# Retention and a gated FFN on one Trainium2 core: g tiles in fourteen places, and smaller last accumulators

## The chip, the core and the metric

The kernel runs on one core of one Trainium2 chip. The metric is device time in microseconds (us); the kernel before takes 590.42 us (median of 3 runs, 590.29 to 590.98). Engines are named as the profile names them: PE (matrix multiply), DVE (vector), ACT (scalar), POOL (GpSimd), SP (the queue that issues nearly all DMAs). Each engine works through its own list of instructions in order, and waits where an instruction's inputs, or the place it writes, are not ready.

## The reference

Attention without softmax, as a recurrence with one decay per head, then two matrix products with a relu6 gate between them:

```python
gamma = 1.0 - 2.0 ** (-5.0 - np.arange(H))
for t in range(S):                       # B, H, S, D = 4, 8, 768, 64
    state = gamma * state + k[:, :, t] (x) v[:, :, t]
    y[:, :, t] = q[:, :, t] @ state / sqrt(D)
x = y as (B*S, H*D) = (3072, 512)
h = x @ w_in                             # w_in 512 x 2048, float64
g = h * clip(h + 3, 0, 6) / 6
out = g @ w_out                          # w_out 2048 x 512, float64
```

All outputs are float32. Both weights come as float64, and have to be turned into float32 on the chip.

## The kernel before

**First phase.** The 3072 tokens are six units (0 to 5) of 512. For each unit, attention makes x, kept as a rounded part and a remainder, so that a product of two such numbers takes three matmuls. Then 16 tiles jj of h are made, one for each 128 columns of w_in: `mm1(u, jj)` does 12 matmuls of 128x512 (4 blocks k, 3 products) into a PSUM tile `h` (three of them in turn), ACT and DVE turn h into `g` (128x512, L468 and L469), and SP stores g to `gd` in DRAM (L470).

**Second phase.** `out` is made with a seven-product scheme (Strassen's, in Winograd's form) over pairs of token tiles and halves of w_out. There are three blocks `sb` of 1024 tokens, each with four groups g of products: (4, 5), (1, 6), (7), (2, 3). A group goes through four steps c: SP loads a tile `gv` of stored g, DVE adds or subtracts into `spare`, ACT and DVE split the operand into its two parts `gc` (L140 and L141), and PE multiplies it by `w2c[2c]` and `w2c[2c + 1]` (L587), 12 matmuls for each product. A step of the first group has two products, so 24 matmuls.

**Weights.** `build_w1` (16 of them) and `build_w2` (16 halves, two for each of the eight tiles w2c[0] to w2c[7]) fetch float64 words into `st` (two buffers), make float32 of them with the five DVE instructions on L122, L123, L128, L131 and L134 and one ACT instruction (L126), with `wb`, `we` and `ww` in one buffer each. A half of w2 then takes four small sums `ws` (L93) and two splits: ACT writes the rounded part into the tile (L140), DVE the remainder (L141), for three blocks from `ww` and four from `ws`. The table WHEN says after which tile of h a half stands in the program: three halves in unit 1, three in unit 2, two each in units 3 and 4, six in unit 5.

**Places.** `wpool` has ten large slots of 14 KB per partition: one of its own ("w0": the first part of w1, later w2c[5]) and nine in rotation ("w"). In program order these hold the early loads of q, k, v and of a decay table, the other four parts of w1, two tiles with x of unit 2, the tiles of w2 and, in the second phase, two `spare`. A tile may be written once the reads of the tile before it in that slot are over. A part of w1 holds 14 of the 64 blocks (jj, k); it is read in every unit, for the last time in unit 5. Part 1 holds blocks 14 to 27, so its last use is jj = 6, k = 3.

**Order.** Only PE's order is written out by hand (`manual_schedule`). The order on the other engines is made when the program is built, by a scheduler that puts an instruction where it expects its inputs and its place to be ready. Second-phase pools lie where the first phase's were: the second `gv` buffer lies over the two `st`, the third over `wb`, `we`, `ww` and `ws`.

Of the kernel before, what the change touches and what calls it, by code (L numbers as in the profile page):

```python
# [19 lines left out]
P = 128  # L20
# [8 lines left out]
def retention_ffn(ctx: ExitStack, tc: tile.TileContext, qkv, w_in, w_out, dvs, dqs, dkc, dqc, dmc, out, B, H, S, D):  # L29
# [14 lines left out]
    UR = 4  # L44
# [96 lines left out]
        nc.vector.tensor_tensor(out=lo, in0=src, in1=hi, op=ALU.subtract)  # L141


    w1s = {}

    def place(shape, dtype, name, own):

        return wpool.tile(shape, dtype, tag="w0" if own else "w", name=name, bufs=1 if own else NSLOT - 1)

    def w1_block(j, k):  # L150
        s, o = divmod(j * NK + k, 14)
# [45 lines left out]
    def load(r):  # L197

        t = rows[r] = {}
        if r < AHEAD and r % 2 == 0:
            early[r] = wpool.tile([P, 7, NPAIR, P], F32, tag="w", name=nm("early"), bufs=NSLOT - 1)
        for i, (x, n) in enumerate((("kt", 1), ("qt", 0), ("vn", 3), ("kn", 2))):
            o = r % 2 * 4 + i
            if r < AHEAD and o < 7:
                t[x] = early[r // 2 * 2][:, o]
            elif x == "kn" and r > CHUNKED and r % 2:
                t[x] = both["am"][:, 1]  # L210
            else:
                tag = SPARE[r // 2] if r < AHEAD else f"l{x}"
                t[x] = apool.tile([P, NPAIR, P], F32, tag=tag, name=nm(x), bufs=BUFS[tag])
            m = NPAIR * P
            if x == "kn" and r % ROWS_B == ROWS_B - 1:
                m = m // 2 if r >= CHUNKED else 0
            if m:
                nc.sync.dma_start(out=t[x].rearrange("p h n -> p (h n)")[:, 0:m], in_=qkv[r, n][:, 0:m])
        if r >= CHUNKED:
            t["vn"], t["kn"] = (  # L220
                t[x].rearrange("p h n -> p (h n)").rearrange("p (c a e) -> p c a e", c=2, e=D) for x in ("vn", "kn")
            )
            scale(r)
        elif r >= AHEAD:
            decay(r)
# [23 lines left out]
    def load_decay(r):  # L249
        if r < AHEAD:  # L250
            if "dq" not in early:
                early["dq"] = wpool.tile([P, ROWS_B, NPAIR, P], F32, tag="w", name=nm("early"), bufs=NSLOT - 1)
            t = early["dq"][:, r % ROWS_B]
        else:
            t = apool.tile([P, NPAIR, P], F32, tag="dq", name=nm("dq"), bufs=1)
        rows[r]["dq"] = t
        if r < ROWS_B or r >= AHEAD:
            nc.sync.dma_start(out=t.rearrange("p h n -> p (h n)"), in_=dqs[r % ROWS_B])
# [75 lines left out]
    def x_place(r):  # L334
        u, n = divmod(r, UR)
        if u not in xs and u == 2:
            xs[u] = [wpool.tile([P, NK, UT], F32R, tag="w", name=nm("x"), bufs=NSLOT - 1) for a in range(2)]
        elif u not in xs:
            x = xpool.tile([P, 2, NK, UT], F32R, tag="x", name=nm("x"))
            xs[u] = [x[:, a] for a in range(2)]  # L340
        return [xs[u][a][:, :, n * P : (n + 1) * P] for a in range(2)]
# [117 lines left out]
    def mm1(u, jj):  # L459
        h = ps_h.tile([P, UT], F32, tag="h", name=nm("h"))  # L460
        for k in range(NK):
            t, o = w1_block(jj, k)
            for n, (a, b) in enumerate(((0, 0), (0, 1), (1, 0))):
                nc.tensor.matmul(  # L464
                    h, t[:, o, a], xs[u][b][:, k], start=k + n == 0, stop=(k, n) == (NK - 1, 2), skip_group_check=True
                )
        g = hpool.tile([P, UT], F32, tag="g", name=nm("g"))
        nc.scalar.activation(out=g, in_=h, func=AF.Relu, bias=three)  # L468
        ins = nc.vector.scalar_tensor_tensor(out=g, in0=g, scalar=6.0, in1=h, op0=ALU.min, op1=ALU.mult)  # L469
        nc.sync.dma_start(out=gd[jj // 2][:, jj % 2, u * UT : (u + 1) * UT], in_=g)  # L470
        return ins.ins
# [10 lines left out]
    for n, (u, jj) in enumerate(steps):  # L482
# [20 lines left out]
        n: ctx.enter_context(tc.tile_pool(name=f"left_{n}", bufs=1, reuse_waits="tile"))  # L503
        for n in ("gv0", "gv1", "gc2", "v", "p", "gc0", "gc1", "q")
    }
    ps_o = [
        ctx.enter_context(tc.tile_pool(name=f"ps_o{i}", bufs=1, space=PSUM, reuse_waits="tile", side=side))
        for i, side in enumerate(("right", "left"))
    ]
    CP = 2  # L510
    TB = 2 * UT
    GROUPS = ((4, 5), (1, 6), (7,), (2, 3))
    spare = [place([P, 14 * BLK], F32, f"spare{i}", False) for i in range(2)]
    sums = [spare[c // 2][:, c % 2 * CP * UT : (c % 2 + 1) * CP * UT].rearrange("p (j n) -> p j n", j=CP) for c in range(4)]
    kept = {n: spare[i][:, 4 * UT : 6 * UT].rearrange("p (h n) -> p h n", h=2) for i, n in enumerate("su")}
    for n in "pqv":
# [19 lines left out]
    def acc6(out_, ps, other):  # L536
        nc.vector.scalar_tensor_tensor(out=out_, in0=ps, scalar=SIXTH, in1=other, op0=ALU.mult, op1=ALU.add)

    def store(sb, t, m, src, h):
        o = out[m * HM : (m + 1) * HM, (2 * sb + t) * UT : (2 * sb + t + 1) * UT].rearrange("(h p) n -> p h n", p=P)  # L540
        nc.sync.dma_start(out=o[:, h], in_=src[:, h])

    for sb in range(NT // TB):
        for g, ids in enumerate(GROUPS):
            acc = {i: ps_o[g % 2].tile([P, 2, UT], F32, tag=f"o{n}", name=nm("o")) for n, i in enumerate(ids)}
            for c in range(NFP // CP):
                with ExitStack() as first:
                    if sb == 0 and g == 0 and c == 0:
                        first.enter_context(tc.high_priority())
                    elif sb == 0 and g == 0:  # L550
                        first.enter_context(tc.issue_after(end))
                    gv = gv_tile()
                    for jj in range(CP):
                        j = c * CP + jj
                        t0 = 2 * sb * UT
                        if g == 0:
                            nc.sync.dma_start(out=gv[:, :, jj], in_=gd[j][:, :, t0 + UT : t0 + TB])
                        elif g == 2:
                            src = gd[j][:, 0, t0 : t0 + TB].rearrange("p (t n) -> p t n", t=2)
                            nc.sync.dma_start(out=gv[:, :, jj], in_=src)  # L560
                        else:
                            nc.sync.dma_start(out=gv[:, 0, jj], in_=gd[j][:, g // 2, t0 : t0 + UT])
                    a, b = gv[:, 0], gv[:, 1]
                    s = sums[c]
                    if g == 0:
                        dve_add(s, a, b)
                        srcs = (b, s)
                    elif g == 1:
                        dve_sub(s, s, a)
                        srcs = (a, s)  # L570
                    elif g == 2:
                        dve_sub(b, a, b)
                        srcs = (b,)
                    else:
                        dve_sub(s, a, s)
                        srcs = (a, s)
                    ops = []
                    for src in srcs:
                        gc = gc_tile()
                        split(gc[:, 0], gc[:, 1], src)  # L580
                        ops.append(gc)
                for i, gc in zip(ids, ops):
                    for h in range(2):
                        for jj in range(CP):
                            j = c * CP + jj
                            for n, (x, y) in enumerate(((0, 0), (0, 1), (1, 0))):
                                nc.tensor.matmul(  # L587
                                    acc[i][:, h],
                                    w2c[j][:, RIGHT[i], x, h],
                                    gc[:, y, jj],  # L590
                                    start=j == 0 and n == 0,
                                    stop=j == NFP - 1 and n == 2,
                                    skip_group_check=True,
                                )
            whole = slice(0, 2)
            if g == 0:
                scaled(kept["p"], acc[4], -SIXTH)
                scaled(kept["q"], acc[5])
            elif g == 1:
                scaled(kept["s"], acc[1])  # L600
                acc6(kept["u"], acc[6], kept["s"])
                dve_add(kept["v"], kept["u"], kept["q"])
            elif g == 2:
                acc6(kept["u"], acc[7], kept["u"])
                dve_add(kept["p"], kept["u"], kept["p"])
                dve_add(kept["q"], kept["u"], kept["q"])
                store(sb, 1, 0, kept["p"], whole)
                store(sb, 1, 1, kept["q"], whole)
            else:
                parts = (whole,) if sb < NT // TB - 1 else (slice(0, 1), slice(1, 2))  # L610
                for k, i, m in (("s", 2, 0), ("v", 3, 1)):
                    for h in parts:
                        acc6(kept[k][:, h], acc[i][:, h], kept[k][:, h])
                        store(sb, 0, m, kept[k], h)
    order.close()


# [95 lines left out]
```

## Time and profile before

| | |
|---|---|
| median of 3 runs | 590.42 us (590.29 to 590.98) |
| the profiled execution | 590.15 us |
| its span, first to last instruction | 588.4 us (1.75 us lie outside) |
| PE busy | 573.7 us (98%), 4604 matmuls |
| DVE busy | 416.6 us (71%) |
| ACT busy | 249.1 us (42%) |
| DMA | 117.05 MB, 199 GB/s on average |
| granted clock, mean | 0.992 |

The profile is one execution. Its views used here are the page, the busy time by window, the timeline of one engine (start, time, engine, line, operation, count, and in brackets the idle time before with what ended it) and the groups by line. A row of the timeline gives how long an instruction takes; instructions of one engine overlap a little, so that the distance from start to start is the time that the engine's list needs.

### The profile page before, as it was taken

What the parts mean: (1) busy time and instruction counts of PE and PEld (TensorE: products, weight loads), DVE (VectorE), ACT (ScalarE), POOL (GpSimd) and SP (SyncE); (2) the same over time, 40 slices, a digit from 0 to 9 for tenths busy, and PEclk for the clock granted to TensorE, in tenths of its full rate; (3) what the DMA queues carried; (4) which work ended last, traced back from release to release, by engine and by line L of the source; (5) the groups of instructions that cost most, each with busy time, mean ns of one, the idle gap of its engine ahead of it and who ended that gap; (6) DMA issues with size and microseconds to landing.
All of it is one profiled execution on the core that took longest, in us unless ns stands there. A gap on an engine that the chain in (4) does not pass through costs nothing.

```text
span 588.4 us, 11368 instructions
## 1 busy us (share of the span) xinstructions
PE 573.7 (98%) x4604; PEld 471.3 (80%) x4604; DVE 416.6 (71%) x588; ACT 249.1 (42%) x393; POOL 35.2 (6%) x39
## 2 busy tenths in 40 slices
PE   8888999999999999999999999999999999999996
PEld 7766788777888888888888888888888888888885
DVE  4879999999533498333225989769587698866871
ACT  5773445443423344332324555444335343344430
POOL 1001000101221121121000000000000000000000
PEclk9988999999999999999999999999999999999999
DMA  8966677665965467555243457564844747635611
GB/s 321 391 234 208 218 254 233 233 216 187 300 231 174 160 225 250 189 182 174 106 135 115 162 194 253 176 218 143 277 152 144 243 143 262 211 114 181 205 72 71
DMA packets 58884, 117.05 MB, mean 199 GB/s; under 512 B 5968, under 2 KB 6352, under 8 KB 58832
## 3 DMA queue, kind: packets, MB, share of 16 engines
q1 hardware_dynamic: 58688, 116.31, 58.7%
q8 instruction: 36, 0.59, 0.4%
q14 instruction: 16, 0.13, 0.1%
q10 hardware_dynamic: 144, 0.02, 0.0%
HBM read 84.85 MB, written 31.46 MB: 198 GB/s over the span
## 4 chain that ended last, share of the span: by engine, by line
PE 78%; DVE 14%; DMA 3%; issue 3%; ACT 1%; SPq 1%; DVEq 0%; ACTq 0%
PE o L587 39%; PE h L464 33%; DVE g L469 2%; DMA st<-in_w_in 2%; PE uz L349 2%; DVE w L141 2%; DVE wb L128 2%; PE sc L349 1%; DVE am L327 1%; DVE we L131 1%; DVE ww L134 1%; PE y L349 1%; DVE we L122 1%; DMA early<-in_qkv 1%; DVE wb L123 1%
## 5 line engine op out<-in xcount | busy, mean ns | idle before, releaser
L464 PE MATMUL h<-x,w 128*128 128x512 f32 x1152 | 271.1, 394 | 2.8 <-DVE x L141 1.2
L464 PEld LDWEIGHTS h<-x,w 128*128 128x128 f32 x1152 | 214.9, 189 | 51.4 <-DVE g L469 3.1
L587 PE MATMUL o<-gc,w 128*128 128x512 f32 x1008 | 231.5, 392 | 0.0
L587 PEld LDWEIGHTS o<-gc,w 128*128 128x128 f32 x1008 | 189.2, 188 | 42.1
L469 DVE SCALAR_TENSOR_TENSOR g<-g,h 128x512 f32<-128x512 f32 x96 | 65.3, 683 | 84.7 <-ACT g L468 84.7
L468 ACT ACTIVATE g<-h,three 128x512 f32<-128x512 f32 x96 | 65.2, 683 | 101.1 <-PE h L464 98.3
L140 ACT ACTIVATE gc<-gv 128x1024 fp32r<-128x1024 f32 x48 | 50.8, 1060 | 65.8 <-PE o L587 55.1
L141 DVE TENSOR_TENSOR gc<-gv,gc 128x1024 fp32r<-128x1024 f32 x48 | 58.6, 1221 | 22.8 <-ACT gc L140 22.7
L140 ACT ACTIVATE gc<-spare 128x1024 fp32r<-128x1024 f32 x36 | 38.2, 1061 | 48.9 <-PE o L587 37.5
L141 DVE TENSOR_TENSOR gc<-spare,gc 128x1024 fp32r<-128x1024 f32 x36 | 43.9, 1220 | 8.6 <-ACT gc L140 8.5
L140 ACT ACTIVATE w<-ww 128x384 fp32r<-128x384 f32 (+2 forms) x34 | 18.7, 555 | 49.0 <-DVE ww L134 46.6
L126 ACT ACTIVATE we<-we,ebias 128x512 int32<-128x512 int32 x32 | 22.9, 717 | 12.2 <-DVE we L122 12.2
L134 DVE SCALAR_TENSOR_TENSOR ww<-wb,we 128x512 f32<-128x512 f32 x32 | 24.5, 765 | 0.6
L235 POOL TENSOR_TENSOR qs<-qt,dq 128x512 f32<-128x512 f32 x12 | 16.7, 1388 | 95.9 <-PE y L349 59.9
L128 DVE SCALAR_TENSOR_TENSOR wb<-st,wb 128x512 f32<-128x512 uint32 x32 | 21.9, 685 | 0.2
L141 DVE TENSOR_TENSOR w<-ww,w 128x384 fp32r<-128x384 f32 (+2 forms) x34 | 19.9, 590 | 3.1 <-ACT w L140 3.1
L131 DVE SCALAR_TENSOR_TENSOR we<-st,we 128x512 int32<-128x512 int32 x32 | 21.9, 683 | 0.0
L96 DVE TENSOR_TENSOR spare<-gv 128x1024 f32<-128x1024 f32 x12 | 14.7, 1222 | 8.0 <-DMA gv<-gd 8.0
L122 DVE TENSOR_SCALAR we<-st 128x512 int32<-128x512 int32 x32 | 14.3, 446 | 8.3 <-DMA st<-in_w_in 8.1
L93 DVE TENSOR_TENSOR spare<-spare,gv 128x1024 f32<-128x1024 f32 x12 | 14.6, 1220 | 5.3 <-DMA gv<-gd 5.3
L93 DVE TENSOR_TENSOR gv<-gv 128x1024 f32<-128x1024 f32 x12 | 14.7, 1223 | 4.6 <-DMA gv<-gd 4.5
L241 ACT ACTIVATE early<-early,cst_sb 128x64 f32<-128x64 f32 x64 | 16.4, 335 | 3.6 <-DMA early<-in_qkv 3.6
(73 smaller groups left out, 395.8 us busy)
## 6 DMA issues: line engine op xcount, KB each, us to landing
gd<-g SPq DMA_DIRECT2D x96, 256.0 KB, 2.7
gv<-gd SPq DMA_DIRECT2D x48, 512.0 KB, 4.9
gv<-gd SPq DMA_DIRECT2D x48, 256.0 KB, 3.1
st<-in_w_in SPq DMA_DIRECT2D x16, 512.0 KB, 4.0
st<-in_w_out SPq DMA_DIRECT2D x16, 512.0 KB, 3.9
early<-in_qkv SPq DMA_DIRECT2D x28, 256.0 KB, 6.0
kt<-in_qkv SPq DMA_DIRECT2D x16, 256.0 KB, 3.8
qt<-in_qkv SPq DMA_DIRECT2D x16, 256.0 KB, 4.2
```

Of the source, the lines that this page charges most:

```text
L93: return nc.vector.tensor_tensor(out=out_, in0=a, in1=b, op=ALU.subtract)
L126: nc.scalar.activation(out=e, in_=e, func=AF.Relu, scale=8.0, bias=ebias)
L128: nc.vector.scalar_tensor_tensor(out=y, in0=lo.bitcast(U32), scalar=2.0**-32, in1=b, op0=ALU.mult, op1=ALU.add)
L131: nc.vector.scalar_tensor_tensor(out=e, in0=hi, scalar=-2147483648, in1=e, op0=ALU.bitwise_and, op1=ALU.bitwise_or)
L134: nc.vector.scalar_tensor_tensor(out=w, in0=y, scalar=2.0**-20, in1=e.bitcast(F32), op0=ALU.mult, op1=ALU.mult)
L140: nc.scalar.activation(out=hi, in_=src, func=AF.Copy)
L141: nc.vector.tensor_tensor(out=lo, in0=src, in1=hi, op=ALU.subtract)
L349: nc.tensor.matmul(out_, lhs, rhs, start=start, stop=True, skip_group_check=True)
L464: nc.tensor.matmul(h, t[:, o, a], xs[u][b][:, k], start=k + n == 0, stop=(k, n) == (NK - 1, 2), skip_group_check=True)
L468: nc.scalar.activation(out=g, in_=h, func=AF.Relu, bias=three)
L469: ins = nc.vector.scalar_tensor_tensor(out=g, in0=g, scalar=6.0, in1=h, op0=ALU.min, op1=ALU.mult)
L587: nc.tensor.matmul(acc[i][:, h], w2c[j][:, RIGHT[i], x, h], gc[:, y, jj], start=j == 0 and n == 0, stop=j == NFP - 1 and n == 2, skip_grou ...
```

## The change

1. The slots are shared out differently: the rotation "w" has seven, and a new one, "wx", has two. "wx" holds the early loads of rows 0 to 3, then the two tiles with x of unit 2, then two `slab`, then the two `spare`. All other tiles, w2c[0] to w2c[7] without w2c[5] among them, rotate through the seven.
2. From unit 3 on, g is not one of three tiles of `hpool` but one of fourteen 512-wide places in the two slabs.
3. In the last group of the last block each accumulator of two banks becomes two tiles of one bank. Each is scaled, added and stored for itself, and the last one in two halves of 256 columns, the second of them stored from ACT's queue.

```diff
     def place(shape, dtype, name, own):
-        return wpool.tile(shape, dtype, tag="w0" if own else "w", name=name, bufs=1 if own else NSLOT - 1)
+        return wpool.tile(shape, dtype, tag="w0" if own else "w", name=name, bufs=1 if own else NSLOT - 3)
+
+    def room(shape, dtype, name, passing):
+        return wpool.tile(shape, dtype, tag="wx" if passing else "w", name=name, bufs=2 if passing else NSLOT - 3)
+
+    def g_place(u, jj):
+        if u < 3:
+            return hpool.tile([P, UT], F32, tag="g", name=nm("g"))
+        n = ((u - 3) * NF + jj) % 14
+        if len(slabs) <= n // 7:
+            slabs.append(room([P, 14 * BLK], F32, nm("slab"), True))
+        return slabs[n // 7][:, n % 7 * UT : (n % 7 + 1) * UT]
...
-            early[r] = wpool.tile([P, 7, NPAIR, P], F32, tag="w", name=nm("early"), bufs=NSLOT - 1)
+            early[r] = room([P, 7, NPAIR, P], F32, nm("early"), r < UR)
...
-            xs[u] = [wpool.tile([P, NK, UT], F32R, tag="w", name=nm("x"), bufs=NSLOT - 1) for a in range(2)]
+            xs[u] = [room([P, NK, UT], F32R, nm("x"), True) for a in range(2)]
...
-        g = hpool.tile([P, UT], F32, tag="g", name=nm("g"))
+        g = g_place(u, jj)
...
-    spare = [place([P, 14 * BLK], F32, f"spare{i}", False) for i in range(2)]
+    spare = [room([P, 14 * BLK], F32, f"spare{i}", True) for i in range(2)]
...
+            last = sb == NT // TB - 1 and g == len(GROUPS) - 1
+            if last:
+                ends.close()
+                ps_e = ctx.enter_context(tc.tile_pool(name="ps_e", bufs=1, space=PSUM, reuse_waits="tile", side="left"))
+            acc = {i: ps_o[g % 2].tile([P, 2, UT], F32, tag=f"o{n}", name=nm("o")) for n, i in enumerate(ids)} if not last else {
+                i: [ps_e.tile([P, UT], F32, tag=f"e{i}{h}", name=nm("o")) for h in range(2)] for i in ids
+            }
...
-                parts = (whole,) if sb < NT // TB - 1 else (slice(0, 1), slice(1, 2))
                 for k, i, m in (("s", 2, 0), ("v", 3, 1)):
-                    for h in parts:
-                        acc6(kept[k][:, h], acc[i][:, h], kept[k][:, h])
-                        store(sb, 0, m, kept[k], h)
+                    if not last:
+                        acc6(kept[k], acc[i], kept[k])
+                        store(sb, 0, m, kept[k])
+                    else:
+                        for h in range(2):
+                            for n in range(2 if (i, h) == (3, 1) else 1):
+                                to = slice(n * BLK, (n + 1) * BLK) if (i, h) == (3, 1) else slice(0, UT)
+                                acc6(kept[k][:, h, to], acc[i][h][:, to], kept[k][:, h, to])
+                                store(sb, 0, m, kept[k], h, to, nc.scalar if n else nc.sync)
```

PE's list is the same in both kernels, row for row. The lists of DVE, ACT and SP are not. The lines of the second kernel are numbered 13 to 20 higher (L469 becomes L482, L557 L577). In the rows below the names end in running numbers; `w_339` and `w_336` are both w2c[3], `w_464` and `w_430` both w2c[5], `w_502` and `w_460` both w2c[7].

DVE, where unit 3 begins, before:

```order
L469 SCALAR_TENSOR_TENSOR g_2379<-g_2379,h_2366 128x512
L141 TENSOR_TENSOR w_339_2553<-ww_2558,w_339_2553 128x3x128
L134 SCALAR_TENSOR_TENSOR ww_2863<-wb_2861,we_2862 128x512
L469 SCALAR_TENSOR_TENSOR g_2396<-g_2396,h_2383 128x512
L141 TENSOR_TENSOR w_339_2553<-ws_2565,w_339_2553 128x4x128
L141 TENSOR_TENSOR w_339_2553<-ww_2863,w_339_2553 128x3x128
L93 TENSOR_TENSOR ws_2870<-ww_2863 128x128 x2
```

and the same place now:

```order
L482 SCALAR_TENSOR_TENSOR g_2379<-g_2379,h_2366 128x512
L482 SCALAR_TENSOR_TENSOR g_2396<-g_2396,h_2383 128x512
L482 SCALAR_TENSOR_TENSOR slab_2413<-slab_2413,h_2400 128x512
L482 SCALAR_TENSOR_TENSOR slab_2413<-slab_2413,h_2417 128x512
L405 TENSOR_TENSOR am_1645<-sc,cmask 128x512
L141 TENSOR_TENSOR x_2502<-y_1644,x_2502 128x4x128
L482 SCALAR_TENSOR_TENSOR slab_2413<-slab_2413,h_2518 128x512
```

The work on w2c[3] that stood between the g's at the end of unit 2 and the start of unit 3 is not there any more.

DVE, in unit 5 (the three g's ahead of the w rows are those of jj = 3, 4, 5, the one behind them that of jj = 6), now:

```order
L482 SCALAR_TENSOR_TENSOR slab_2705<-slab_2705,h_3639 128x512
L482 SCALAR_TENSOR_TENSOR slab_2705<-slab_2705,h_3676 128x512
L482 SCALAR_TENSOR_TENSOR slab_2705<-slab_2705,h_3692 128x512
L141 TENSOR_TENSOR w_336_2550<-ww_2555,w_336_2550 128x3x128
L141 TENSOR_TENSOR w_336_2550<-ws_2562,w_336_2550 128x4x128
L134 SCALAR_TENSOR_TENSOR ww_2853<-wb_2851,we_2852 128x512
L482 SCALAR_TENSOR_TENSOR slab_2705<-slab_2705,h_3728 128x512
```

The rows of w2c[3] stand here now, behind the g of jj = 5. Before, the first w rows of unit 5 were those of w2c[5], behind the g of jj = 2.

DVE, at the last half of w2, before:

```order
L469 SCALAR_TENSOR_TENSOR g_3941<-g_3941,h_3928 128x512
L93 TENSOR_TENSOR ws_3973<-ws_3973,ww_3966 128x128
L141 TENSOR_TENSOR w_502_3907<-ww_3966,w_502_3907 128x3x128
L141 TENSOR_TENSOR w_502_3907<-ws_3973,w_502_3907 128x4x128
L96 TENSOR_TENSOR spare_4050<-gv_4057 128x1024
L469 SCALAR_TENSOR_TENSOR g_3958<-g_3958,h_3945 128x512
L141 TENSOR_TENSOR gc_4064<-spare_4050,gc_4064 128x1024
L469 SCALAR_TENSOR_TENSOR g_3995<-g_3995,h_3982 128x512
L469 SCALAR_TENSOR_TENSOR g_4012<-g_4012,h_3999 128x512
L96 TENSOR_TENSOR spare_4050<-gv_4091 128x1024
```

and DVE and SP now (`st_3918` is the last half's fetch, `gv_4045` and `gc_4049` belong to step c = 1 of the second phase's first group):

```order
L128 SCALAR_TENSOR_TENSOR wb_3920<-st_3918,wb_3920 128x512
L131 SCALAR_TENSOR_TENSOR we_3921<-st_3918,we_3921 128x512
L134 SCALAR_TENSOR_TENSOR ww_3922<-wb_3920,we_3921 128x512
L93 TENSOR_TENSOR ws_3929<-ww_3922 128x128 x2
L93 TENSOR_TENSOR ws_3929<-ww_3922,ws_3929 128x128
L141 TENSOR_TENSOR w_460_3865<-ww_3922,w_460_3865 128x3x128
L93 TENSOR_TENSOR ws_3929<-ws_3929,ww_3922 128x128
L141 TENSOR_TENSOR w_460_3865<-ws_3929,w_460_3865 128x4x128
L96 TENSOR_TENSOR spare_4004<-gv_4045 128x1024
L141 TENSOR_TENSOR gc_4049<-gv_4045,gc_4049 128x1024
L141 TENSOR_TENSOR gc_4052<-spare_4004,gc_4052 128x1024
```

```order
L111 DMA st_3813<-in_w_out 128x512
L483 DMA gd_70<-slab_2413 128x512
L111 DMA st_3866<-in_w_out 128x512
L582 DMA gv_4219<-gd_67 128x512
L582 DMA gv_4219<-gd_68 128x512
L111 DMA st_3918<-in_w_out 128x512
L577 DMA gv_4045<-gd_65 128x2x512
L577 DMA gv_4045<-gd_66 128x2x512
L577 DMA gv_4079<-gd_67 128x2x512
L577 DMA gv_4079<-gd_68 128x2x512
```

Before, the last half of w2 was followed on DVE by the work of step c = 0 and by the g's of the last three tiles of unit 5. Now all of unit 5's g's stand ahead of it, step c = 1 follows right behind it, and on SP the load of step c = 1 stands behind the last fetch.

More of the change, by code (lines that the diff above doesn't have):

```diff
@@ L141, in split @@
         nc.vector.tensor_tensor(out=lo, in0=src, in1=hi, op=ALU.subtract)
-    w1s = {}
+    w1s, slabs = {}, []
     def place(shape, dtype, name, own):
-        return wpool.tile(shape, dtype, tag="w0" if own else "w", name=name, bufs=1 if own else NSLOT - 1)
+        return wpool.tile(shape, dtype, tag="w0" if own else "w", name=name, bufs=1 if own else NSLOT - 3)
[8 more added lines that the diff above has]
+        return slabs[n // 7][:, n % 7 * UT : (n % 7 + 1) * UT]
     def w1_block(j, k):
@@ L251, in load_decay @@
             if "dq" not in early:
-                early["dq"] = wpool.tile([P, ROWS_B, NPAIR, P], F32, tag="w", name=nm("early"), bufs=NSLOT - 1)
+                early["dq"] = room([P, ROWS_B, NPAIR, P], F32, nm("early"), False)
             t = early["dq"][:, r % ROWS_B]
@@ L505, in retention_ffn @@
     }
+    ends = ctx.enter_context(ExitStack())
     ps_o = [
-        ctx.enter_context(tc.tile_pool(name=f"ps_o{i}", bufs=1, space=PSUM, reuse_waits="tile", side=side))
+        ends.enter_context(tc.tile_pool(name=f"ps_o{i}", bufs=1, space=PSUM, reuse_waits="tile", side=side))
         for i, side in enumerate(("right", "left"))
@@ L537, in acc6, with store @@
         nc.vector.scalar_tensor_tensor(out=out_, in0=ps, scalar=SIXTH, in1=other, op0=ALU.mult, op1=ALU.add)
-    def store(sb, t, m, src, h):
+    def store(sb, t, m, src, h=slice(0, 2), to=slice(0, UT), eng=nc.sync):
         o = out[m * HM : (m + 1) * HM, (2 * sb + t) * UT : (2 * sb + t + 1) * UT].rearrange("(h p) n -> p h n", p=P)
-        nc.sync.dma_start(out=o[:, h], in_=src[:, h])
+        eng.dma_start(out=o[:, h, to], in_=src[:, h, to])
     for sb in range(NT // TB):
         for g, ids in enumerate(GROUPS):
-            acc = {i: ps_o[g % 2].tile([P, 2, UT], F32, tag=f"o{n}", name=nm("o")) for n, i in enumerate(ids)}
+            last = sb == NT // TB - 1 and g == len(GROUPS) - 1
[5 more added lines that the diff above has]
+            }
             for c in range(NFP // CP):
@@ L587, in retention_ffn @@
                                 nc.tensor.matmul(
-                                    acc[i][:, h],
+                                    acc[i][h] if last else acc[i][:, h],
                                     w2c[j][:, RIGHT[i], x, h],
@@ L594, in retention_ffn @@
                                 )
-            whole = slice(0, 2)
             if g == 0:
@@ L606, in retention_ffn @@
                 dve_add(kept["q"], kept["u"], kept["q"])
-                store(sb, 1, 0, kept["p"], whole)
-                store(sb, 1, 1, kept["q"], whole)
+                store(sb, 1, 0, kept["p"])
+                store(sb, 1, 1, kept["q"])
             else:
-                parts = (whole,) if sb < NT // TB - 1 else (slice(0, 1), slice(1, 2))
                 for k, i, m in (("s", 2, 0), ("v", 3, 1)):
-                    for h in parts:
-                        acc6(kept[k][:, h], acc[i][:, h], kept[k][:, h])
-                        store(sb, 0, m, kept[k], h)
+                    if not last:
[7 more added lines that the diff above has]
+                                store(sb, 0, m, kept[k], h, to, nc.scalar if n else nc.sync)
     order.close()
```

## The prediction

> **What bounds the kernel now.** I read the page's busy times first, then the busy time by window.
>
> ```profile
> span 588.4 us, 11368 instructions
> PE 573.7 (98%) x4604; PEld 471.3 (80%) x4604; DVE 416.6 (71%) x588; ACT 249.1 (42%) x393; POOL 35.2 (6%) x39
> PE   8888999999999999999999999999999999999996
> ...
> 200.00:230.00 30.00, 29.91 (x352) 24.70 (x352) 26.99 (x55) 14.59 (x27) 5.93 (x4) 1.00 0.63 207
> 230.00:260.00 30.00, 29.73 (x352) 24.56 (x352) 10.26 (x16) 9.09 (x16) 4.65 (x4) 1.00 0.65 227
> ...
> 352.44:583.95 231.51, 231.48 (x1009) 189.01 (x1007) 174.83 (x151) 95.79 (x92) 0.00 (x0) 1.00 0.55 180
> ```
>
> The columns of a window are its length, then busy time and count of PE, weight loads, DVE, ACT and POOL, then granted clock, DMA share and GB/s. PE sets the time: from 200 to 260 it lacks 0.36 us of work, in the second phase 0.03. A free place for g can give back no more than those 0.36 us, since waits on DVE or ACT that PE does not feel cost nothing. What is left to win is the tail behind the last matmul; what can be lost is PE's cover. So the next view is the timeline where the phases meet.
>
> ```profile
> 303.35 49.26 PE L464 MATMUL h<-x,w 128*128 128x512 f32 x216
> 352.44 7.81 PE L587 MATMUL o<-gc,w 128*128 128x512 f32 x33
> 317.28 0.69 ACT L468 ACTIVATE g<-h,three 128x512 f32<-128x512 f32 x1 [2.03 <-PE h L464]
> 318.64 0.53 ACT L140 ACTIVATE w<-ww 128x384 fp32r<-128x384 f32 x1 [0.67 <-PE h L464]
> 319.20 0.56 DVE L141 TENSOR_TENSOR w<-ww,w 128x384 fp32r<-128x384 f32 x1 [0.51 <-ACT w L140]
> 328.16 0.69 ACT L468 ACTIVATE g<-h,three 128x512 f32<-128x512 f32 x1 [2.03 <-PE h L464]
> ```
>
> PE goes from the first phase (49.09 us for 216 matmuls, so 0.2273 each and 2.73 a tile) to the second without a gap. Unit 5's 192 matmuls begin at 352.44 - 43.64 = 308.8; its tile 2 is done at 317.28, tile 6 at 328.16. The row at 318.64 shows a split of w2 waiting for PE, not for data: w2c[5] goes where part 0 of w1 lay, whose last block is used in the middle of tile 3. So a tile of w2 that follows a part of w1 waits for unit 5.
>
> **The change part by part.** *The places.* The seven slots of "w" get, in program order, two early loads, the decay table, four parts of w1, then w2c[0], [1], [2] in the slots of the first three. The next, w2c[3], follows part 1 of w1, which is read until tile 6 of unit 5; before, it followed x of unit 2. The order lists bear this out: its splits left the start of unit 3 and stand behind tile 5's g in unit 5. Everything behind them is held too, since `ww` and `ws` have one buffer. So ten halves of w2 (bar the first half up to its sums, and the second up to L131) fall behind 328.16, where six halves were done before, and those from 319.2 on. What does a half cost?
>
> ```profile
> L469 DVE SCALAR_TENSOR_TENSOR g<-g,h 128x512 f32<-128x512 f32 x10 | 6.8, 681 | 0.0
> L134 DVE SCALAR_TENSOR_TENSOR ww<-wb,we 128x512 f32<-128x512 f32 x5 | 3.4, 687 | 0.1
> L128 DVE SCALAR_TENSOR_TENSOR wb<-st,wb 128x512 f32<-128x512 uint32 x4 | 2.7, 684 | 0.0
> ...
> 320.33 0.68 DVE L134 SCALAR_TENSOR_TENSOR ww<-wb,we 128x512 f32<-128x512 f32 x1
> 342.49 0.68 DVE L469 SCALAR_TENSOR_TENSOR g<-g,h 128x512 f32<-128x512 f32 x1
> 343.09 0.68 DVE L128 SCALAR_TENSOR_TENSOR wb<-st,wb 128x512 f32<-128x512 uint32 x1
> 343.81 0.69 DVE L134 SCALAR_TENSOR_TENSOR ww<-wb,we 128x512 f32<-128x512 f32 x1
> 345.21 0.69 DVE L469 SCALAR_TENSOR_TENSOR g<-g,h 128x512 f32<-128x512 f32 x1
> 346.80 0.69 DVE L141 TENSOR_TENSOR w<-ws,w 128x512 fp32r<-128x512 f32 x1 [0.23 <-ACT w L140]
> 347.40 1.22 DVE L96 TENSOR_TENSOR spare<-gv 128x1024 f32<-128x1024 f32 x1
> 363.06 1.22 DVE L141 TENSOR_TENSOR gc<-gv,gc 128x1024 fp32r<-128x1024 f32 x1
> 364.20 1.22 DVE L93 TENSOR_TENSOR spare<-spare,gv 128x1024 f32<-128x1024 f32 x1
> ```
>
> The first three rows are the groups of the stretch 319.1 to 347.45. From the `ww` at 320.33 to the `spare` at 347.40 DVE runs without a break: 27.07 us for four whole halves, the later part (from `ww`) of a fifth, and ten g's. A g takes 0.60 from start to start (342.49 to 343.09), ten 6.0. The later part is what runs from 343.81 to 347.40 without one g in between (345.21), 2.99 at most; without its wait, 2.6 to 2.8. That leaves 27.07 - 6.0 - 2.6 = 18.5, **4.6 us a half**. An instruction on 1024 columns takes 1.14 (363.06 to 364.20).
>
> By the changed list DVE has, from the first split of w2c[3] to the last of w2c[7]: two splits (1.1), the later part of a half (2.6), eight whole halves (36.8), ten g's (6.0), and `spare` and `gc` of steps c = 0 and c = 3 (four, 4.6): 51.1 us. It begins at 328.16 + 0.56 (318.64 to 319.20) = 328.7 and ends at 379.8. Before, the last split of w2 ended at 347.4.
>
> Who waits for it: PE's step c = 0 needs w2c[0] and [1] and an operand ahead of most of this, and runs from 352.44 for 24 matmuls (231.51 / 1008 = 0.2297 each) to 357.95. Step c = 1 cannot follow: its `gc` stands on DVE behind the last half, and on SP its load stands behind the last fetch and goes where `st` lies, so it waits for the last reads of `st` (L131), about 2.7 us before the list's end: 377.1.
>
> ```profile
> gv<-gd SPq DMA_DIRECT2D x48, 512.0 KB, 4.9
> ...
> st<-in_w_out SPq DMA_DIRECT2D x16, 512.0 KB, 3.9
> ...
> L140 ACT ACTIVATE gc<-gv 128x1024 fp32r<-128x1024 f32 x48 | 50.8, 1060 | 65.8 <-PE o L587 55.1
> ...
> 354.46 1.20 SPq L557 DMA_DIRECT2D gv<-gd  x2
> 361.92 1.23 DVE L96 TENSOR_TENSOR spare<-gv 128x1024 f32<-128x1024 f32 x1 [0.80 <-DMA gv<-gd]
> ```
>
> Two loads: 0.6 for the second issue (1.20 for two), 4.9 to landing (bounds: 3.9, the fetch of the same size, and 361.92 - 354.46 = 7.5 in a crowded place). Then ACT's part (1.06) and DVE's (1.22), with 0.1 between: 377.1 + 0.6 + 4.9 + 2.4 = 385.0. PE stands still from 357.95 to 385.0: **27.0 us**. Its h tiles in unit 5 may come free a little later too, with the g's between the halves; but c = 0 could end 27 us later without moving c = 1, so this adds nothing.
>
> *The restart.* After so long a pause the array is slow at first.
>
> ```profile
> 33.00:34.00 1.00, 1.00 (x4) 0.81 (x3) 0.96 (x3) 0.00 (x0) 0.00 (x0) 0.50 0.24 90
> 34.00:35.00 1.00, 1.00 (x3) 0.72 (x3) 0.33 (x1) 0.00 (x0) 0.00 (x0) 0.50 0.03 10
> ...
> 31.65 3.99 PE L464 MATMUL h<-x,w 128*128 128x512 f32 x11 [0.99 <-DVE x L141]
> ```
>
> After short pauses at 30 us the granted clock was 0.50 for some 3 us, and 11 matmuls took 3.99 us instead of 2.50: **1.5 us** (bounds 0 and twice that). The Trainium skill, "TensorE: Matmul & The Clock Gate", Part 1, says that the clock halves after an idle window of about 3.4 us and comes back after about as long a stretch of work. By it the restart costs 1.7, and the sum is 0.2 higher; the trace agrees in size, though here shorter pauses were enough.
>
> *The tail.*
>
> ```profile
> 559.80 24.13 PE o L587 x105
> 583.96 1.29 DVE L537 SCALAR_TENSOR_TENSOR kept_v<-o,kept_v 128x512 f32<-128x512 f32 x2 [1.43 <-PE o L587]
> 584.67 0.93 SPq L541 DMA_DIRECT2D out<-kept_v  x2
> out<-kept_v SPq DMA_DIRECT2D x2, 256.0 KB, 2.1
> L93 DVE TENSOR_TENSOR ws<-ww x32: 277/284/1021, 107.2 to 344.7; 128x128 f32<-128x128 f32 x32
> ```
>
> Both halves of the last accumulator wait for the last matmul (583.93), though the first is complete six matmuls earlier. With a tile a bank, only 2 x 256 columns come behind it. One of 256 lies between 0.28 (128 columns) and 0.68 (512), say 0.42; the two end at +0.8 instead of +1.3. The store is half as large; it saves 0 to 0.6 of its 2.1, I take 0.2. **-0.7 us** (bounds -0.5 and -1.1). The gain from units 3 to 5 is 0 to -0.36; I take 0, for DVE was not late there.
>
> Sum on the profiled execution: 588.4 + 27.0 + 1.5 - 0.7 = 616.2 of span, and 1.75 outside it (590.15 - 588.4): 617.95. The median of the runs shown, 590.42, is 0.05% above that execution. I predict **618 us**.
>
> **The rivals.** *Fetches bind the halves.* From the last read of `st` to the next use of that buffer the list has about 6.5 us (one half and 2 us); a fetch needs 0.3 to issue and 3.9 to land, so it is hidden. For it: SP's list puts some of these fetches behind `gv` loads, and landings reach 7.5. Then the six halves fetched in the stretch are 1.5 us late each: 627. Against: before, fetches issued in the same stretch never stopped DVE.
>
> *A second stall.* The load of step c = 2 waits for the last split of w2 and lands about 3 us behind that of c = 1; c = 2 is due 5.5 to 7 us behind c = 1. For it: DVE then also has group 1's rows in between. If it lands as late as 7.5, PE waits some 3 us more: 621.
>
> *The list is hidden after all* (the other side). If unit 5 and step c = 0 covered the 51.1 us, PE would feel nothing, and tail and places would give 590.15 - 0.7 - 0.36 = 589.1. That decides from the point where a half costs under 1.2 us: the list would have to end 5.2 us (385.0 - 379.8) ahead of 357.95, so within 24.0 us, of which all but the eight halves takes 14.3. For it speaks that six halves were hidden before; against it that DVE ran them back to back, and that they began 9 us earlier. The same time would follow if w2c[3] got another place than the lists show.
>
> **How the numbers follow.** The forecast has 0.76, the fetches 0.11, the second stall 0.10, the hidden list 0.03. The likeliest case's own range: low with 4.46 a half (the rows without any wait, -1.1), 3.9 to landing (-1.0), no slow restart (-1.5), and -1.1 at the tail (-0.4), 614; high with a wait of 0.23 more in each half (+1.8) and 7.5 to landing (+2.6), 622.4. I give 613 to 625, which takes in the second stall and part of the fetches. About 0.2% is what a measurement of this kernel can tell from no change: faster 0.02, within it 0.01, slower 0.97, the first two out of the hidden list.
>
> **What would show it.** PE idle once, for 25 to 29 us, in front of step c = 1 of the first group; DVE without a break from about 328.7 to 380, and w2's L134 rows up to there; the `gv` load issued near 377; the granted clock at 0.50 for some 3 us behind the stall; units 3 and 4 as long as before; the last stores ending about 3.8 us behind the last matmul instead of 4.5. It is wrong if DVE idles inside its list (fetches), if PE stops again before the first group ends, or if the first split of w2c[3] comes before tile 6 is done.

## The result and the profile after

The changed kernel takes **616.53 us** (median of 5 runs, 615.79 to 618.91); the kernel before, run beside it, 590.42 us (median of 5, 589.33 to 592.45). The ratio is 1.0446, 95% interval 1.0416 to 1.0477: slower by 26.1 us, where the forecast was 618.0 us in a range of 613 to 625. The profiled execution of the changed kernel is the slowest of the five: 618.91 us, with a span of 617.2.

The page of the changed kernel, its span and busy times, two of the rows of 40 slices (one slice is 15.4 us), and the shares of the chain that ended last; behind the dots the last two of these from the page of before:

```profile
span 617.2 us, 11321 instructions
PE 577.2 (94%) x4604; PEld 472.8 (77%) x4604; DVE 415.6 (67%) x589; ACT 249.8 (40%) x393; POOL 35.0 (6%) x39
PE   8898999999999999999999920999999999999997
PEclk9988999999999999999999975899999999999999
PE 70%; DVE 21%; DMA 4%; issue 2%; ACT 1%; SPq 1%; DVEq 0%; ACTq 0%
...
PEclk9988999999999999999999999999999999999999
PE 78%; DVE 14%; DMA 3%; issue 3%; ACT 1%; SPq 1%; DVEq 0%; ACTq 0%
```

Most of the loss is one hole in slices 24 and 25 ("2" and "0"); PE is also busy 3.5 us longer for the same 4604 matmuls. In the chain that ended last, DVE's share went from 14% to 21% and PE's from 78% to 70%. The granted clock (`PEclk`) is lower in the hole and behind it. The timeline of PE around the hole (start, time, what, count, idle time before with what ended it):

```profile
303.18 46.54 PE L477 MATMUL h<-x,w 128*128 128x512 f32 x204
350.08 3.02 PE L477 MATMUL h<-x,w 128*128 128x512 f32 x12 [0.36 <-DVE slab L482]
352.93 5.76 PE L607 MATMUL o<-gc,w 128*128 128x512 f32 x24
383.76 0.79 PE L607 MATMUL o<-gc,w 128*128 128x512 f32 x1 [25.07 <-ACT gc L140]
385.08 37.16 PE L607 MATMUL o<-gc,w 128*128 128x512 f32 x149 [0.52 <-DVE gc L141]
```

After the 24 matmuls of step c = 0 PE stands still for 25.07 us, does the first matmul of c = 1, waits 0.52 us for DVE's part of the same operand, and then runs without another stop. What DVE did meanwhile, as groups by line and shape from the first split of w2c[3] (328.55) to the end of the last one (380.5), the rows that count the parts, and then its timeline at the end with SP's row of the same moment:

```profile
L141 DVE TENSOR_TENSOR w<-ws,w 128x512 fp32r<-128x512 f32 x10 | 6.9, 690 | 0.8 <-ACT w L140 0.7
L482 DVE SCALAR_TENSOR_TENSOR slab<-slab,h 128x512 f32<-128x512 f32 x10 | 6.8, 680 | 0.0
L134 DVE SCALAR_TENSOR_TENSOR ww<-wb,we 128x512 f32<-128x512 f32 x9 | 6.2, 687 | 0.1
L122 DVE TENSOR_SCALAR we<-st 128x512 int32<-128x512 int32 x8 | 3.4, 420 | 0.0
L96 DVE TENSOR_TENSOR spare<-gv 128x1024 f32<-128x1024 f32 x2 | 2.4, 1221 | 0.5 <-DMA gd<-slab 0.5
...
328.55:380.50 51.95, 29.78 (x130) 23.87 (x128) 50.39 (x111) 23.70 (x39) 0.00 (x0) 0.84 0.47 152
```

```profile
376.27 0.68 DVE L131 SCALAR_TENSOR_TENSOR we<-st,we 128x512 int32<-128x512 int32 x1
...
379.77 0.69 DVE L141 TENSOR_TENSOR w<-ws,w 128x512 fp32r<-128x512 f32 x1 [0.69 <-ACT w L140]
382.66 1.23 DVE L96 TENSOR_TENSOR spare<-gv 128x1024 f32<-128x1024 f32 x1 [2.20 <-DMA gv<-gd]
...
376.98 4.69 SPq L577 DMA_DIRECT2D gv<-gd  x4
```

The list holds what the forecast counted: splits of ten halves, L134 of nine, the reads of `st` (L122) of eight, ten g's, two `spare`. DVE is busy for 50.39 of 51.95 us. The load for c = 1 is issued at 376.98, right behind the last read of `st` (376.27 + 0.68), and its data end DVE's 2.20 us of waiting at 382.66.

Units 3 and 4, and the tail:

```profile
200.00:230.00 30.00, 30.00 (x354) 24.88 (x353) 8.96 (x13) 8.33 (x14) 4.64 (x4) 1.00 0.58 195
230.00:260.00 30.00, 30.00 (x354) 24.86 (x353) 9.17 (x14) 9.40 (x16) 4.66 (x4) 1.00 0.51 175
...
604.73 8.88 PE L607 MATMUL o<-gc,w 128*128 128x512 f32 x38
613.65 0.76 DVE L551 SCALAR_TENSOR_TENSOR kept_v<-o,kept_v 128x256 f32<-128x256 f32 x2 [0.67 <-PE o L607]
614.44 0.35 ACTq L555 DMA_DIRECT2D out<-kept_v  x1
```

In the first window DVE's busy time fell from 26.99 to 8.96 us: the halves of w2 left it, and PE has no hole there any more. At the end the last matmul is over at 613.61, and the span ends 3.6 us later.

### The profile page after: what moved, and what is told of

Read it like the earlier page. It is cut to its first block, busy times and chain, and to the rows that moved or that the text cites. A ratio compares the mean times of both kernels' runs of the same rounds, so it can differ in the third digit from the quotient of the medians.

```text
span 617.2 us, 11321 instructions
## 1 busy us (share of the span) xinstructions
PE 577.2 (94%) x4604; PEld 472.8 (77%) x4604; DVE 415.6 (67%) x589; ACT 249.8 (40%) x393; POOL 35.0 (6%) x39
## 4 chain that ended last, share of the span: by engine, by line
PE 70%; DVE 21%; DMA 4%; issue 2%; ACT 1%; SPq 1%; DVEq 0%; ACTq 0%
PE o L607 37%; PE h L477 28%; DVE w L141 3%; DVE g L482 2%; DVE wb L128 2%; DVE we L131 2%; DVE ww L134 2%; DMA st<-in_w_in 2%; DVE ws L93 2%; PE uz L362 2%; PE sc L362 1%; DVE am L340 1%; DVE we L122 1%; PE y L362 1%; DVE wb L123 1%
## 5 line engine op out<-in xcount | busy, mean ns | idle before, releaser
L607 PE MATMUL o<-gc,w 128*128 128x512 f32 x1008 | 235.1, 395 | 25.6 <-ACT gc L140 25.1
L607 PEld LDWEIGHTS o<-gc,w 128*128 128x128 f32 x1008 | 191.2, 190 | 69.3 <-ACT gc L140 25.5
L482 DVE SCALAR_TENSOR_TENSOR slab<-slab,h 128x512 f32<-128x512 f32 x48 | 32.9, 686 | 72.5 <-ACT slab L481 72.5
L481 ACT ACTIVATE slab<-h,three 128x512 f32<-128x512 f32 x48 | 32.8, 686 | 78.5 <-PE h L477 78.5
L482 DVE SCALAR_TENSOR_TENSOR g<-g,h 128x512 f32<-128x512 f32 x48 | 32.7, 683 | 35.3 <-ACT g L481 35.3
L481 ACT ACTIVATE g<-h,three 128x512 f32<-128x512 f32 x48 | 32.4, 680 | 41.2 <-PE h L477 41.1
L134 DVE SCALAR_TENSOR_TENSOR ww<-wb,we 128x512 f32<-128x512 f32 x32 | 23.3, 727 | 0.6
L131 DVE SCALAR_TENSOR_TENSOR we<-st,we 128x512 int32<-128x512 int32 x32 | 21.9, 684 | 0.0
L122 DVE TENSOR_SCALAR we<-st 128x512 int32<-128x512 int32 x32 | 15.1, 471 | 8.3 <-DMA st<-in_w_in 8.1
```

Of the source, the lines that this page charges most:

```text
L131: nc.vector.scalar_tensor_tensor(out=e, in0=hi, scalar=-2147483648, in1=e, op0=ALU.bitwise_and, op1=ALU.bitwise_or)
L134: nc.vector.scalar_tensor_tensor(out=w, in0=y, scalar=2.0**-20, in1=e.bitcast(F32), op0=ALU.mult, op1=ALU.mult)
L607: nc.tensor.matmul(acc[i][h] if last else acc[i][:, h], w2c[j][:, RIGHT[i], x, h], gc[:, y, jj], start=j == 0 and n == 0, stop=j == NFP - ...
```

## The experiments

The theory was that three things make up the difference: the later place of w2c[3] and w2c[4] (the stall and the restart behind it), the tail, and nothing from the places of g. The first four kernels take these apart; the next three look at the restart. The kernel before ran beside each: 591.63 us (median of 23) beside the first four, 590.42 (of 11) beside the next two, 590.34 (of 7) beside the last.

**The tail alone.** The slots and g as before, with the changed last group:

```diff
-        return wpool.tile(shape, dtype, tag="w0" if own else "w", name=name, bufs=1 if own else NSLOT - 3)
+        return wpool.tile(shape, dtype, tag="w0" if own else "w", name=name, bufs=1 if own else NSLOT - 1)
...
-        return wpool.tile(shape, dtype, tag="wx" if passing else "w", name=name, bufs=2 if passing else NSLOT - 3)
+        return wpool.tile(shape, dtype, tag="w", name=name, bufs=NSLOT - 1)
...
     def g_place(u, jj):
-        if u < 3:
+        if True:
```

> The slots and the g tiles of before, with the last group's tile a bank and its last half in two pieces. By the theory (the slots cause the loss, the tail gives back 0.7 to 0.9 us) PE runs from the first phase into the second without a stop, the last stores end about 3.6 us behind the last matmul instead of 4.5, and the time is 589.6 us. If the last group's tiles themselves cost something (another order of the operands, a wait in front of the last group), the time is above 590.4 and PE shows an idle time in the last group.

Measured: 590.37 us, ratio 0.9986 (0.9968 to 1.0004). The interval reaches past 1, so the tail cannot be told from no change by the time. Its PE timeline, at the phase boundary and at the end:

```profile
354.05 68.32 PE L607 MATMUL o<-gc,w 128*128 128x512 f32 x297
...
569.79 15.74 PE L607 MATMUL o<-gc,w 128*128 128x512 f32 x68
585.57 0.76 DVE L551 SCALAR_TENSOR_TENSOR kept_v<-o,kept_v 128x256 f32<-128x256 f32 x2 [0.67 <-PE o L607]
```

There is no stall between c = 0 and c = 1. The last matmul ends at 585.53, and the span of 589.1 ends 3.6 us later, against 4.5 before: the 0.9 us is there in the profile.

**The slots alone.** Slots and tail as changed, but g in its three tiles throughout:

```diff
     def g_place(u, jj):
-        if u < 3:
+        if True:
```

> The slots shared out as in the change, but g stays in three tiles and no slab exists; the last group as in the change. By the theory the loss comes from w2c[3] following part 1 of w1, so it stays. DVE's list from the first split of w2c[3] to the last of w2c[7] is two instructions of 1.14 shorter than with the slabs, since the spare of step c = 0 need not wait for a slab and now stands ahead of the list: the stall ends 2.3 us sooner, 614.2 us. If the g places cause the loss (their waits, or where g is written), the time returns to about 590.

Measured: 615.31 us, ratio 1.0403 (1.0370 to 1.0437). The places of g are not what costs. Its timeline of PE and the window of its list on DVE, which runs from 326.52 to 375.95:

```profile
350.24 5.76 PE L607 MATMUL o<-gc,w 128*128 128x512 f32 x24
379.20 0.79 PE L607 MATMUL o<-gc,w 128*128 128x512 f32 x1 [23.20 <-ACT gc L140]
380.52 41.73 PE L607 MATMUL o<-gc,w 128*128 128x512 f32 x173 [0.52 <-DVE gc L141]
...
326.52:375.95 49.43, 29.48 (x130) 23.96 (x128) 48.23 (x109) 22.99 (x38) 0.00 (x0) 0.84 0.44 140
```

The list is 2.5 us shorter than with the slabs (49.43 against 51.95, and 51.92 in the second profile of the change, which follows below) and holds 109 instructions of DVE instead of 111. The groups of this window have one `spare` and one `gc` where the change has two of each, and two such instructions at 1.14 are 2.3 us. In the change `spare` lies where the slabs are, and one of the two waits for the last stores of g out of them (the 0.5 us "<-DMA gd<-slab" above). So the slabs do lengthen the list a little; in the medians, 615.31 against 616.53 and 615.89, that cannot be told from their spread.

**The two tiles of w2 put back.** As the slots alone, but w2c[3] and w2c[4] follow x of unit 2 again, in "wx", and `spare` takes two of the seven:

```diff
-        w2c[j] = place([P, 7, 2, 2, P], F32R, nm("w2"), j == 5)
+        w2c[j] = room([P, 7, 2, 2, P], F32R, nm("w2"), True) if j in (3, 4) else place([P, 7, 2, 2, P], F32R, nm("w2"), j == 5)
...
-    spare = [room([P, 14 * BLK], F32, f"spare{i}", True) for i in range(2)]
+    spare = [room([P, 14 * BLK], F32, f"spare{i}", False) for i in range(2)]
```

> As r2_slots_only, but w2c[3] and w2c[4] follow the x of unit 2 in the slots that pass, and the two spare rotate in the seven. By the theory that takes the whole loss away: DVE's list is again that of the kernel before, and with the new tail the time is 589.6 us. If sharing the slots out in two rotations costs by itself, the time stays above 600.

Measured: 591.20 us, ratio 0.9994 (0.9970 to 1.0018). The whole loss is gone with these two tiles, and PE goes through the boundary without a stop:

```profile
339.65 16.25 PE L477 MATMUL h<-x,w 128*128 128x512 f32 x71
355.75 66.50 PE L607 MATMUL o<-gc,w 128*128 128x512 f32 x289
```

It came out 1.6 us above what was expected. In its profile the second phase starts 3.3 us later than in before's; a part of that is taken up below.

**One slab.** g gets seven places in one slab, w2c[3] goes back behind x of unit 2, and w2c[4] now follows part 1 of w1. (In the change it follows a later part: its first split on ACT waits for PE until 337.51 there, and starts at 326.31 here.) Two halves leave the list:

```diff
-        n = ((u - 3) * NF + jj) % 14
+        n = ((u - 3) * NF + jj) % 7
...
-        w2c[j] = place([P, 7, 2, 2, P], F32R, nm("w2"), j == 5)
+        w2c[j] = room([P, 7, 2, 2, P], F32R, nm("w2"), True) if j == 3 else place([P, 7, 2, 2, P], F32R, nm("w2"), j == 5)
...
-    spare = [room([P, 14 * BLK], F32, f"spare{i}", True) for i in range(2)]
+    spare = [room([P, 14 * BLK], F32, f"spare{i}", i == 0) for i in range(2)]
```

> One slab of seven places for g, w2c[3] in the other slot that passes; w2c[4] still follows part 1 of w1. By the theory two of the ten halves go back to unit 3: DVE's list behind tile 6 of unit 5 is 41.9 us instead of 51.1, so it ends near 370.6, PE stands 9.2 us less, and with the same slow restart the time is 607.3 us. If the loss is all or nothing (any tile that waits for w1 costs the same pause, for instance because the fetches or the load of step c = 1 set its end), the time is within 3 us of 616.5; if only w2c[3] matters, it is near 590.

Measured: 611.52 us, ratio 1.0344 (1.0308 to 1.0380), 4.2 us above what was expected: less is gained than the list lost. Its timelines, DVE's list first and last, then PE, then SP:

```profile
326.86 0.56 DVE L141 TENSOR_TENSOR w<-ww,w 128x384 fp32r<-128x384 f32 x1 [1.86 <-ACT w L140]
368.41 0.69 DVE L141 TENSOR_TENSOR w<-ws,w 128x512 fp32r<-128x512 f32 x1 [0.70 <-ACT w L140]
374.45 1.22 DVE L96 TENSOR_TENSOR spare<-gv 128x1024 f32<-128x1024 f32 x1 [5.34 <-DMA gv<-gd]
...
358.14 0.80 PE L607 MATMUL o<-gc,w 128*128 128x512 f32 x1 [4.60 <-ACT gc L140]
375.54 0.80 PE L607 MATMUL o<-gc,w 128*128 128x512 f32 x1 [11.50 <-ACT gc L140]
376.86 45.48 PE L607 MATMUL o<-gc,w 128*128 128x512 f32 x190 [0.52 <-DVE gc L141]
...
366.47 0.80 SPq L582 DMA_DIRECT2D gv<-gd  x2
367.37 2.94 SPq L577 DMA_DIRECT2D gv<-gd  x4
```

The list takes 42.2 us (326.86 to 369.1), 9.7 less than in the change, which is two halves at 4.6 and some. But the data for c = 1 come 5.34 us after its end instead of 2.20. The last read of `st` is over at 363.33 here (L131, 362.65 + 0.68), but the load was issued only at 367.37: on SP it stands behind a load of another step (L582), which went out at 366.47, when DVE had made `gc` of c = 3 (365.22, 1.23 us long). So it left 1.73 us ahead of the list's end, where the change has 3.48, and its data took 7.08 us to reach DVE instead of 5.68; why they took longer is not shown. Together that took 3.1 us of the gain away. (The first hole, 4.60 us, is in front of the second operand of c = 0, whose rows also stand inside the list; it ends long before c = 1 could go on.) So the term "a half of w2 costs 4.6 us of stall" holds on DVE, and reaches PE only as far as the load can follow.

**The change again, and with PE kept at work in the pause.** The restart was the term known worst: 1.5 us, from a case with much shorter pauses. Is it the clock, or are operands late? The same kernel was run once more, and once with matmuls between c = 0 and c = 1, whose results nothing reads:

```diff
+                    if sb == 0 and g == 0 and c == 1:
+                        dummy = ps_o[1].tile([P, 2, UT], F32, tag="o0", name=nm("o"))
+                        for _ in range(96):
+                            nc.tensor.matmul(dummy[:, 0, 0:P], mask[:, 0, 0], mask[:, 0, 0], start=True, stop=True)
```

> The change once more, beside r5_warm on the same chip: 616.5 us. Its runs spread over 3 us so far, against 1 to 3 for the kernel before; if the spread comes from how long the clock stays low behind the pause, the profile's span less the time at half clock is the same as in the first profile of the change, and r5_warm spreads less.

> The change, with 96 matmuls of 128x128 on a constant between steps c = 0 and c = 1 of the first group (about 24 us by the 0.25 us that such a matmul took at the start of the program; their result goes to a place that is cleared later). They fill the pause and change nothing else in the lists. If the slow clock sets the price of the restart, the granted clock stays at 1.0 behind the pause, step c = 1 begins where it did, and the time is 2.9 us lower than the change's, 613.6 us. If the steps behind the pause are held by the supply from DVE and ACT instead, the time stays within 0.7 us of the change's.

Measured: 615.89 us for the change again (ratio 1.0435, 1.0390 to 1.0481), and 615.92 us with the 96 matmuls (ratio 1.0425, 1.0388 to 1.0463): no difference. But the 96 ended too early, so the question stayed open. PE with the 96 (each shows as two matmuls), and the granted clock in its windows:

```profile
355.76 21.60 PE L570 MATMUL o<-mask 128*128 128x128 f32 x192
380.80 0.79 PE L611 MATMUL o<-gc,w 128*128 128x512 f32 x1 [3.44 <-ACT gc L140]
...
358.00:377.00 19.00, 19.00 (x173) 19.00 (x172) 18.03 (x42) 6.45 (x11) 0.00 (x0) 1.00 0.31 102
383.00:385.00 2.00, 2.00 (x6) 1.52 (x6) 2.00 (x3) 1.57 (x2) 0.00 (x0) 0.50 0.80 260
```

One took 0.225 us (21.60 / 96), 0.025 less than reckoned. After a pause of only 3.44 us the clock was at 0.50 all the same. So the pause was closed with more of them:

```diff
-                        for _ in range(96):
+                        for _ in range(112):
```

> The run before it with 112 instead of 96 matmuls of 128x128 between steps c=0 and c=1 of the first group; they compute nothing that is used. At the 0.225 us that one of the 96 took, they last 25.2 us and end within about half a microsecond of the moment the list in front of c=1 is done (PE had been idle 3.44 us there). If the granted clock behind the pause is what the restart costs, the clock stays at 1.00 from 385 to 390 us, and the matmuls behind c=1 run at 0.2297 us each from the first: 1.7 to 2.9 us less than in the change, an estimate of about 613.5 us. If the operands' supply behind the pause is what it costs, the same 2 us are lost with the clock at 1.00, and the time stays at about 616.

Measured: 614.12 us, ratio 1.0406 (1.0360 to 1.0452); by time alone the 1.8 us below the change lie within the spread of both. The profile decides, PE's timeline and two windows behind c = 1:

```profile
356.16 25.17 PE L570 MATMUL o<-mask 128*128 128x128 f32 x224
381.55 0.50 PE L611 MATMUL o<-gc,w 128*128 128x512 f32 x1 [0.21 <-ACT gc L140]
382.86 37.39 PE L611 MATMUL o<-gc,w 128*128 128x512 f32 x162 [0.81 <-DVE gc L141]
...
384.00:386.00 2.00, 2.00 (x11) 1.65 (x10) 2.00 (x3) 1.59 (x2) 0.00 (x0) 1.00 0.73 250
PEclk9999999999999999999999999999999999999999
```

The clock stays at 1.00, and 162 matmuls take 37.39 us, 0.2308 each, from the first. From the moment c = 1 goes on (its second matmul) to the end of the span, PE's work is the same in each of these kernels. The last column is the mean granted clock in the 10 us from that moment:

| kernel | c = 1 goes on | to the end of the span | above the kernel with 112 | clock |
|---|---|---|---|---|
| the change | 385.08 | 232.12 | 2.8 | 0.71 |
| the change again | 382.74 | 230.86 | 1.5 | 0.84 |
| slots alone | 380.52 | 231.08 | 1.7 | 0.81 |
| one slab | 376.86 | 231.14 | 1.8 | 0.83 |
| with 96 matmuls | 382.12 | 231.38 | 2.0 | 0.78 |
| with 112 matmuls | 382.86 | 229.34 | 0 | 1.00 |

What the clock lacks of 1.00 in these 10 us is 2.9, 1.6, 1.9, 1.7 and 2.2 us of work, the loss in the column before to within 0.2; in the 215 us behind them the clock is 1.00 in all six. So the restart costs 1.5 to 2.8 us, and with the clock kept up it costs nothing: operands are not late. Why the half clock lasts longer in one execution than in another is not settled.

```profile
385.00:390.00 5.00, 4.92 (x12) 3.86 (x13) 5.00 (x6) 2.11 (x2) 0.00 (x0) 0.50 0.44 129
...
385.00:390.00 5.00, 5.00 (x21) 4.07 (x20) 5.00 (x6) 2.27 (x3) 0.00 (x0) 0.90 0.46 142
```

The first row is the window from 385 to 390 of the change, clock 0.50 and 12 matmuls; the second the same window of the change again, 0.90 and 21. The second one's c = 1 came 2.34 us earlier, its half clock ended about 5 us earlier.

## Why the prediction was right, step by step

**Where w2c[3] goes, and what is held behind it: right.** The first split of w2c[3] came at 328.55, where 328.7 was worked out, behind tile 6 of unit 5. That the places of w2c[3] and w2c[4] are the cause is shown by the kernel with the two tiles put back: 591.20 us.

**The list of 51.1 us: right to 2%.** It took 51.9 and ended at 380.46 instead of 379.8. The prediction had left waits out of its halves; DVE waited 0.46 for a store out of a slab and 0.69 for ACT ahead of the last split, so its parts were a little too long to make up for that.

**The load and its landing: right.** Issued at 376.98 (377.1 foretold), data for DVE at 382.66 (382.6). That the moment of issue fits so well is partly luck: the list ended 0.7 later than worked out, and the last read of `st` stood 0.8 further ahead of its end (3.48 us between issue and end instead of 2.7).

**The stall: right.** PE went on with c = 1 at 385.08, where 385.0 was foretold. In the execution before, c = 0 would have been followed at 357.95, so this is 27.1 us of the 27.0. PE itself stood still for less, 25.07 + 0.52 = 25.6 us; the rest is a second phase that began 0.5 us later (352.93 against 352.44), 0.25 more for c = 0, and the first matmul of c = 1, which ran as soon as ACT's part was there, 0.79.

**The restart: mechanism right, size too small.** The prediction took 1.5 us, with bounds of 0 and 3; the runs show 1.5 to 2.8, and 2.8 in the profiled execution. The upper end of the likeliest case's own range, 622.4, was added up without the 3. And the place at 31 us that gave the price ran at a clock of 1.00 in another execution (2.76 us, last section), so that 1.5 came as near as it did is partly luck. The estimate from the page "TensorE: Matmul & The Clock Gate", Part 1, of the Trainium skill was 1.7, nearer to most of these rows. It also says that the window in which activity is counted runs freely, so that the number of slow matmuls differs between runs of one kernel; that agrees with 1.5 in one execution and 2.8 in another, though no row here shows the window itself.

**The tail: right, a little small.** 0.9 us instead of 0.7, in the change and alone. DVE's last two instructions end 0.80 us behind the last matmul (+0.8 foretold); the store behind them saved 0.4 us instead of 0.2.

**Nothing for units 3 to 5: too little.** This is the step that failed. The prediction saw 0.36 us of holes in PE and took 0 for them, with 0.36 as the most. In the change both windows are full (30.00 of 30.00), and the 0.36 was one execution's. The three kernels that keep halves of w2 in units 3 and 4 as before all have a hole in the attention of that stretch, of different length (the rows are of before, of the tail alone, and of the kernel with w2 put back):

```profile
237.02 0.28 PE L349 MATMUL uz<-vn,am 64*64 64x64 f32 x2 [0.27 <-issue]
238.55 0.27 PE L362 MATMUL uz<-vn,am 64*64 64x64 f32 x2 [1.23 <-POOL qs L248]
238.56 0.27 PE L362 MATMUL uz<-vn,am 64*64 64x64 f32 x2 [2.03 <-issue]
```

Behind the 2.03 the clock was also below 1.00 for a while (0.94 as the mean of 230 to 260). In the change, in its second profile, with the slots alone and with the 96 and 112 matmuls, both windows are full. A single profile of before could not show that the hole is often longer than 0.27, so the gain there is about 0.4 to 2.1 us (what PE lacks in the two windows of the three kernels) and not 0. Why halves of w2 on DVE lead to this hole is not shown. The gain may be one reason why the median lies 1.5 us under the forecast; the profiled execution, which has it too, lies 0.9 over it.

**The sum.** On the profiled execution: 27.1 for the stall, 2.8 for the restart, -0.9 for the tail, -0.2 for the one matmul of c = 1 that ran ahead of its second part make 28.8, and 588.4 + 28.8 = 617.2, its span.

**The rivals.** Fetches that bind the halves did not come: DVE idled 1.6 us in the list (51.95 - 50.39), and the row that reads a fetched tile first waited for nothing (L122, 0.0). There is no second stall: from 385.08 PE runs on. The list was not hidden. Faster or no change, 0.03 in all, would have needed what the kernel with the two tiles put back does.

## What to carry to other kernels

When tiles that rotate through common slots are divided into two rotations, write down for every tile which tile it now follows and when that one is read for the last time; here, room for g put two weight tiles behind parts of w1 that are read until the last unit. The price is then read from one engine's list: the instructions that cannot start before that moment, at their distance from start to start, against the work that is left to cover them, and then the order on the queue that loads what comes next. And where several single profiles of one kernel differ by a few us, take a small hole in one of them as a sample, not as a bound.

## What the runs showed that was not expected

- Executions of one kernel differ by some us, and in large part with the clock. Of before's 11 runs beside the change again, the two with a mean granted clock of 1.000 took 588.5 and 588.7 us, the two at 0.991 took 593.5 and 593.9; 0.9% of 588 us is 5.3. It is not the clock alone: of those at 0.994 one took 590.4 and one 593.7. One place of it is the short pauses in the first units. At 31 us the same 11 matmuls took 3.99 us in before's profile, and in the change's two profiles

```profile
31.59 4.28 PE L477 MATMUL h<-x,w 128*128 128x512 f32 x11 [0.98 <-DVE x L141]
...
31.39 2.76 PE L477 MATMUL h<-x,w 128*128 128x512 f32 x11 [0.98 <-DVE x L141]
```

  with the same wait of 0.98 us ahead. The first execution starts its second phase at 352.93, the second at 350.88. A difference of 2 us between two single profiles tells nothing about an edit here, unless the profiles show where it arises.
- How little the clock needs shows in front of c = 1: with 3.44 us of idle time, one matmul and 0.52 us more it stood at 0.50 (it fell some 2.4 us into the pause: 1.00 up to 379.5, 0.71 as the mean of the next half us, 0.50 behind it); with 0.21 us, one matmul and 0.81 us it stayed at 1.00.
- A load can be late because of work that it has nothing to do with: with one slab, the load of c = 1 waited on SP behind one that was waiting for DVE, and a list shorter by 9.7 us gave back 6.5 of it (from the list's start to where c = 1 goes on: 376.86 - 326.86 = 50.0 us, in the change 385.08 - 328.55 = 56.5).
